# The first half of k loaded as fp32 over two other queues, with three small edits beside it: windowed attention and a gated feed-forward on one core

## The chip, the cores and the metric

The kernel runs on one core of one Trainium2 chip. The metric is the device time of one execution in microseconds (us); of several executions the median counts.

## The reference

The inputs are fp32: q, k and v of 8 batches, 8 heads, 576 positions and head size 64, and two weights.

```python
scores = q @ k.T / sqrt(64)                       # per batch and head
scores = where(|i - j| <= 32, scores, -1e9)       # a window of 32 to each side
x = (softmax(scores) @ v), heads side by side     # 4608 tokens x 512
h = x @ w_in                                      # 512 -> 2048
g = where(h >= 1, h, where(h <= -1, 0, (h + 1)**2 / 4))
out = g @ w_out                                   # 2048 -> 512
```

## The kernel before

**Two jobs in one stream.** All work is in bf16. Attention makes xT, the normalized attention output with tokens along the columns, batch by batch. The feed-forward goes over blocks of 256 tokens (18 blocks) in eight steps of 256 hidden columns. The main loop counts these steps as `a` (a = 8 x block + step): each does eight hp matmuls (L504), then ScalarE and VectorE turn hp into gT (L508 to L516). Attention pieces are hung between the steps by a table written by hand, `at(a, ...)`; each engine runs its instructions in the order in which the program gives them.

**The product with w_out** for the first two blocks is cut into sixteen pieces, `pair(x)` (L460): piece x = 0 to 3 takes block 0, output columns 0 to 255, and w_out rows 512x to 512x + 511 (row groups k = 4x to 4x + 3). The list `pairs` says behind which step a each piece goes.

**Loads.** The inputs come in by DMA. GpSimd issues nearly all of them, and these DMAs cast fp32 to bf16 on the way: `load_half` (L85), `load_v` (L106), `load_w_in` (L110), `load_w_out` (L115), `load_rows` (L92) and `load_nat` (L98). GpSimd's order is: the first half of batch 0's k, two DMAs; the small mask operation (L131); v of batch 0, four DMAs; w_in columns 0 to 511, four; the second half of q and k, four; w_in on; w_out rows k = 0 to 3; the last w_in; three mask copies (L151, L153); the rest of w_out's first 256 columns, and batch 1. [...]

**The first stretch** up to step a = 0 is a chain: load q and k, transpose them on TensorE (L187 for tiles in two parts, 18 matmuls; L189 for a cast tile, 9), copy them out of PSUM (L190, one part on ScalarE and one on VectorE), scores (L206 masks, L227 products), exponentials on ScalarE (L235), sums and products with v (L293), 1/sum by a logarithm and an exponential on ScalarE (L299, L300), the product on VectorE (L305), then hp. Idle places of TensorE are filled with dummy matmuls (L336).

Of the kernel before, what the change touches and what calls it, by code (L numbers as in the profile page):

```python
# [7 lines left out]
FP = mybir.dt.float32  # L8
# [6 lines left out]
def kernel(  # L15
# [19 lines left out]
    nc = tc.nc  # L35
    B, H, S, D = q.shape
# [40 lines left out]
    qn, kn, vn = {}, {}, {}  # L77
    HD = (slice(0, 64), slice(64, 128))

    def load_half(half, t, h, eng=None, x=None):  # L80

        src, dst, nm = ((q, qn, "qh"), (k, kn, "kh"))[t]
        if (0, half) not in dst:
            dst[0, half] = early.tile([128, 2, S], BF, name=nm, tag=nm, bufs=2) if x is None else x
        (eng or nc.gpsimd).dma_start(out=dst[0, half][:, h], in_=src[0].rearrange(  # L85
            "(h y) (l p j) d -> h l p y (j d)", h=2, l=2, p=32)[h][half])
# [29 lines left out]
                            in_=moe_w_out.rearrange("(ko ki) f -> ki ko f", ki=128)[:, k0:k1, 256 * c:256 * c + 256])  # L116

    early = ctx.enter_context(tc.tile_pool(name="early", bufs=1))
    q32 = early.tile([128, 2, S], FP, name="q32")
    for h in range(2):  # L120
        load_half(0, 0, h, (nc.sync, nc.scalar)[h], q32)
    for h in range(2):
        load_half(0, 1, h)
    A.preload_act_table_set("natural_log_exp_and_others")
    warm = const.tile([128, 512], BF, name="warm")
    V.memset(warm, 0.0)
# [15 lines left out]
    def put(todo):  # L142
        for fn, *x in todo:
            fn(*x)
# [7 lines left out]
    for m, n, x in ((mask4, 8, 128), (mask8, 4, TAIL)):  # L152
        P.tensor_copy(m.rearrange("p (n j) -> p n j", n=n),  # L153
                      band[:, :x].rearrange("p (n j) -> p n j", n=1).to_broadcast([128, n, x]))
    put([(load_w_out, 0, k, k + 4) for k in range(4, 16, 4)] + [(load_rows, 1, t) for t in range(2)])
    put([(load_v, 1, n) for n in range(4)] + [(load_w_out, 1, 8 * n, 8 * n + 8) for n in range(2)])
    put([(load_nat, 2, t) for t in range(2)] + [(load_v, 2, n) for n in range(4)])

# [3 lines left out]
    def qkT(b, t):  # L162
        if t == 0:
            return qTs[b % 3][:, PAD:]
        if b not in kT:
            kT[b] = ktp.tile([128, NY * S], BF, name="kT")
        return kT[b]

    def tpose(b, n, t, copy, ps):


        half, part = divmod(n, 2)
        j0, j1 = ((0, 5), (5, 9))[part]
        if b:
            src = qn[b] if t == 0 else kn[b]
            src = [src[:, half + 2 * h] for h in range(2)]
            dst = qkT(b, t).rearrange("d (y e p j) -> d y e p j", y=2, e=2, j=9)[:, half, :, :, j0:j1]
            like = "d j (e p) -> d e p j"
        else:
            src = (qn, kn)[t][b, half]  # L180
            src = src if src.shape[1] == 9 else [src[:, h] for h in range(2)]
            dst = qkT(b, t).rearrange("d (y l p j) -> d l y p j", l=2, p=32, j=9)[:, half, :, :, j0:j1]
            like = "d j (p y) -> d y p j"
        for j in range(j0, j1):
            if isinstance(src, list):
                for h in range(2):
                    nc.tensor.transpose(ps[HD[h], j - j0], src[h][:, D * j:D * j + D], ident)  # L187
            else:
                nc.tensor.transpose(ps[:, j - j0], src[:, j], ident)  # L189
        return lambda: copy(dst, ps[:, :j1 - j0].rearrange(like, p=64 if b else 32))  # L190
# [20 lines left out]
    def scores(b, ys, pars, cs, eng, pool=ps_s, w=128):  # L211

        if b not in pt:
            pt[b] = ptp.tile([128, 2, 2, 2, 512], BF, name="pt")
        ps = two_banks(pool)
        n = 0
        if eng is None:
            cols = (ys[1] - ys[0]) * (pars[1] - pars[0]) * (cs[1] - cs[0])
            add_mask([ps[:, h] for h in range(2)], cols, w)
        for y1 in range(*ys):  # L220
            for par in range(*pars):
                for c2 in range(*cs):
                    c = 2 * c2 + par
                    for a in range(2):
                        for h in range(2):
                            s0 = S * (y1 + 2 * a) + 64 * c
                            nc.tensor.matmul(ps[HD[a], h, w * n:w * n + w], kT[b][HD[h], s0:s0 + 64],  # L227
                                             qTs[b % 3][HD[h], PAD + s0 - 32:PAD + s0 - 32 + w],
                                             start=eng is not None, stop=True, skip_group_check=True)
                    n += 1  # L230
        p = pt[b][:, :, ys[0]:ys[1], pars[0]:pars[1], 128 * cs[0]:128 * cs[1] - 128 + w]
        m = 2 if n > cs[1] - cs[0] else 1
        p = p[:, :, ys[0] - ys[0]] if ys[1] - ys[0] == 1 else p[:, :, :, 0]
        like = "p h (y j) -> p h y j"
        A.activation(p, ps[:, :, :w * n].rearrange(like, y=m), AF.Exp, scale=D ** -0.5)  # L235
        mask(eng, p, mask4[:, :256 * n].rearrange("p (h j) -> p h j", h=2).rearrange(like, y=m))
# [81 lines left out]
    def tp1(pool):  # L318
        if pool is ps_h:
            return pool.tile([128, 8, 128], BF, name="tp", tag="hp")  # L320
        return pool.tile([128, 2, 8, 128], BF, name="tp", tag="bb")[:, 0]
# [10 lines left out]
    def keep_warm(n, pool, tag):  # L332

        z = pool.tile([128, 512], FP, name="z", tag=tag)
        for _ in range(n):
            nc.tensor.matmul(z, warm[:, :128], warm, start=True, stop=True)  # L336

    def cast(x, nm, cut):

        y = early.tile([128, 9, 2, D], BF, name=nm)  # L340
        o, i = y.rearrange("p j h d -> p h j d"), x.rearrange("p h (j d) -> p h j d", d=D)
        V.tensor_copy(o[:, :, :cut], i[:, :, :cut])
        A.copy(o[:, :, cut:], i[:, :, cut:])
        return y.rearrange("p j h d -> p j (h d)")

    with tc.tile_pool(name="ps_p", bufs=1, space=bass.MemoryType.PSUM) as ps_p:
        keep_warm(11, ps_h, "hp")

        V.memset(qkT(0, 0).rearrange("d (y s) -> d y s", y=NY)[:, :, S // 2:352], 0.0)
        for b in range(LONG):  # L350
            V.memset(qkT(b, 0).rearrange("d (y s) -> d y s", y=NY)[:, :, S - PAD:], 0.0)
        V.memset(qkT(0, 1).rearrange("d (y s) -> d y s", y=NY)[:, :, S // 2:320], 0.0)
        qn[0, 0] = cast(q32, "qb", 5)
        qq = [tpose(0, n, 0, (A.copy, V.tensor_copy)[n], tp1(ps_h)) for n in range(2)]
        for x in qq:
            x()
        kk = [tpose(0, n, 1, (A.copy, V.tensor_copy)[n], tp1((ps_n, ps_p)[n])) for n in range(2)]
        keep_warm(3, ps_h, "hp")
        for x in kk:
            x()  # L360
        scores(0, (0, 1), (0, 2), (0, 2), None)
        scores(0, (0, 2), (0, 1), (2, 3), None, ps_n, 32)
        scores(0, (1, 2), (0, 2), (0, 2), None, ps_p)
        keep_warm(4, ps_h, "hp")
        e0 = sums(0, 0, 0, TB)
        keep_warm(2, ps_h, "hp")
        e1 = sums(0, 1, 0, TB, ps_p)
        keep_warm(7, ps_h, "hp")
        e0()
        e1()  # L370
# [4 lines left out]

    NB = NT // TB
    NF = DFF // 256
    pairs = [(6, 0), (7, 1), (9, 2), (10, 3), (11, 4), (12, 5), (15, 6), (15, 8), (16, 7), (17, 9)]
    two_on_act = (1, 7, 8, 9, 10, 11, 12)
    ev = {}  # L380

# [100 lines left out]
    for a in range(NF * NB + NF):  # L482
        t, f = divmod(a, NF)
# [70 lines left out]
```

The softmax here doesn't subtract the row's maximum and nothing guards it: scores larger than these inputs give would overflow.

## Time and profile before

| | |
|---|---|
| median of 6 runs | 309.28 us (308.47 to 309.68) |
| the profiled execution | 309.21 us |
| its span, first to last instruction | 307.4 us, so 1.81 us lie around it |
| TensorE (PE) busy | 299.5 us, 97% |
| VectorE (DVE), ScalarE (ACT), GpSimd (POOL) busy | 242.1, 192.8, 77.4 us |

In timelines a row gives its start, its length, engine, line, operation, out<-in, count, and in brackets the idle time of the engine before it with what ended that. PEld are weight loads, POOL rows of DMA are issues (the transfer lands later), and DMA rates count the bytes written, so that a transfer that casts fp32 to bf16 reads twice the rate shown.

### The profile page before, as it was taken

To read this page: it belongs to the slowest core of one execution; us is meant where nothing else is said; L and a number is where in the kernel's file an instruction comes from. 1 tells how busy PE (TensorE), PEld (TensorE's weight loads), DVE (VectorE), ACT (ScalarE), POOL (GpSimd) and SP (SyncE) were. 2 spreads that over 40 slices of the span, in tenths; PEclk is the share of its full clock that TensorE was granted. 3 is DMA by queue.
4 is the path that set the end of the run, shared out by engine and by line. 5 is a ranking of instruction groups with operands and counts; after the bars stand their busy time and mean duration, and the time that the engine had idled before them with its cause. 6 is when DMAs were issued, how large, how long until landed. Compare 5 with 4: busy or idle time off the path is not lost.

```text
span 307.4 us, 8496 instructions
## 1 busy us (share of the span) xinstructions
PE 299.5 (97%) x3650; PEld 206.4 (67%) x3650; DVE 242.1 (79%) x376; ACT 192.8 (63%) x320; POOL 77.4 (25%) x92
## 2 busy tenths in 40 slices
PE   7979999999999999999999999999999999999995
PEld 3558878876666666666666666666666666666654
DVE  4278568978888888889888888889888888888760
ACT  4687886747856667566656666566676666554431
POOL 8798461018007205500460003700000000000000
PEclk9999999999999999999999999999999999999999
DMA  9999999999999997996799056990820011010111
GB/s 150 183 194 189 179 201 155 170 161 130 146 210 80 169 190 93 172 99 143 106 169 136 33 107 98 163 146 28 170 56 36 34 36 36 35 36 34 58 47 68
DMA packets 137174, 35.70 MB, mean 116 GB/s; under 512 B 122161, under 2 KB 132913, under 8 KB 137137
## 3 DMA queue, kind: packets, MB, share of 16 engines
q0 software_dynamic: 102976, 18.06, 82.6%
q1 hardware_dynamic: 34016, 16.81, 25.6%
q8 instruction: 28, 0.46, 0.6%
q10 hardware_dynamic: 144, 0.29, 0.4%
q14 instruction: 10, 0.07, 0.1%
HBM read 36.70 MB, written 9.44 MB: 150 GB/s over the span
## 4 chain that ended last, share of the span: by engine, by line
PE 90%; DMA 4%; POOL 3%; ACT 1%; issue 1%; DVE 0%; POOLq 0%; ACTq 0%
PE hp L504 39%; PE op L444 36%; PE bb L293 6%; PE op L460 4%; DMA w_in<-in_moe_w_in_dram 4%; PE bb L227 2%; PE op L433 1%; POOL vn L106 1%; POOL w_in L110 1%; PE tp L187 1%; ACT pt L235 1%; POOL kh L85 0%; DVE gT L513 0%; ACT mx L512 0%; PE bb L252 0%
## 5 line engine op out<-in xcount | busy, mean ns | idle before, releaser
L504 PE MATMUL hp<-xT,w_in 128*128 128x256 bf16 x1152 | 149.4, 273 | 2.4 <-DMA w_in<-in_moe_w_in_dram 1.1
L508 ACT ACTIVATE rr<-hp 128x512 f32<-128x512 f32 x144 | 85.7, 595 | 88.6 <-PE hp L504 88.5
L504 PEld LDWEIGHTS <-w_in 128*128 128x128 bf16 x1152 | 112.0, 98 | 41.8 <-issue 2.3
L444 PE MATMUL op<-w_out,gT 128*128 128x512 bf16 x496 | 126.9, 380 | 0.0
L515 DVE TENSOR_TENSOR mx<-hp,rr 128x512 f32<-128x512 f32 x137 | 94.5, 689 | 31.1 <-ACT rr L508 29.2
L516 DVE SCALAR_TENSOR_TENSOR gT<-rr,mx 128x512 bf16<-128x512 f32 x137 | 95.2, 695 | 4.7
L444 PEld LDWEIGHTS <-gT 128*128 128x128 bf16 x496 | 46.1, 98 | 34.8
L98 POOL DMA_DIRECT2D qn<-in_q_dram x12 | 14.6, 1223 | 111.7 <-DMA kT<-kn 107.7
L235 ACT ACTIVATE pt<-bb 128x1024 bf16<-128x1024 f32 (+1 forms) x33 | 32.7, 1002 | 4.6 <-PE bb L227 3.2
L305 DVE TENSOR_TENSOR xT<-bb,rc 128x512 bf16<-128x512 f32 (+1 forms) x32 | 21.0, 657 | 10.2 <-ACT rc L300 9.6
L106 POOL DMA_DIRECT2D vn<-in_v_dram x32 | 27.5, 893 | 4.9 <-DMA w_out<-in_moe_w_out_dram 3.7
L300 ACT ACTIVATE rc<-lr 128x512 f32<-128x512 f32 (+2 forms) x40 | 23.5, 587 | 1.3
L449 ACT COPY osb<-op 128x512 f32<-128x512 f32 x31 | 18.1, 583 | 8.7 <-PE op L444 8.3
L299 ACT ACTIVATE lr<-bb 128x512 f32<-128x512 f32 (+2 forms) x40 | 22.0, 551 | 0.4 <-PE bb L293 0.4
L201 DVE TENSOR_TENSOR pt<-pt,mask 128x1024 bf16<-128x1024 bf16 (+1 forms) x33 | 20.2, 613 | 0.5 <-ACT pt L235 0.5
L293 PE MATMUL bb<-pt,ones 64*64 64x256 bf16 (+3 forms) x352 | 19.6, 256 | 0.1
L293 PE MATMUL bb<-pt,vn 64*64 64x128 bf16 (+3 forms) x712 | 18.4, 204 | 0.2 <-DMA vn<-in_v_dram 0.2
L293 PEld LDWEIGHTS <-vn 64*64 64x64 bf16 x712 | 16.7, 107 | 0.4 <-DMA vn<-in_v_dram 0.4
L460 PE MATMUL op<-w_out,gT 128*128 128x256 bf16 x128 | 16.5, 273 | 0.0
L293 PEld LDWEIGHTS <-ones 64*64 64x64 bf16 x352 | 10.2, 105 | 8.9 <-issue 8.9
L98 POOL DMA_DIRECT2D kn<-in_k_dram x12 | 14.6, 1234 | 0.2
L460 PEld LDWEIGHTS <-gT 128*128 128x128 bf16 x128 | 12.0, 98 | 1.9
(59 smaller groups left out, 115.5 us busy)
## 6 DMA issues: line engine op xcount, KB each, us to landing
out_dram<-osb SPq DMA_DIRECT2D x35, 256.0 KB, 2.4
vn<-in_v_dram POOLq DMA_DIRECT2D x32, 144.0 KB, 10.5
qn<-in_q_dram POOLq DMA_DIRECT2D x12, 288.0 KB, 7.0
kn<-in_k_dram POOLq DMA_DIRECT2D x12, 288.0 KB, 9.4
w_in<-in_moe_w_in_dram POOLq DMA_DIRECT2D x12, 128.0 KB, 6.1
w_out<-in_moe_w_out_dram POOLq DMA_DIRECT2D x4, 256.0 KB, 7.3
w_out<-in_moe_w_out_dram POOLq DMA_DIRECT2D x2, 512.0 KB, 15.4
kh<-in_k_dram POOLq DMA_DIRECT2D x4, 144.0 KB, 5.3
```

Source lines behind the costliest of these rows:

```text
L98: nc.gpsimd.dma_start(out=x[:, :, h], in_=src[b, NY * h:NY * h + NY].rearrange("y s d -> (y s) d") .rearrange("(u p) d -> p u d", p=128))
L106: nc.gpsimd.dma_start(out=vn[b][64 * a:64 * a + 64, :, h], in_=v[b, y:y + 2].rearrange("y s d -> (y s) d") .rearrange("(c r) d -> r c d", ...
L235: A.activation(p, ps[:, :, :w * n].rearrange(like, y=m), AF.Exp, scale=D ** -0.5)
L293: nc.tensor.matmul(bb[HD[h], a, o + c0:o + c1], ones[HD[a]] if c is None else vn[b][HD[a], c, h], p(a, h), start=n == 0, stop=True, skip_g ...
L299: A.activation(lr[:, :, :D0], bb[:, :, D0:2 * D0], AF.Ln)
L300: A.activation(rc[:, :, :D0], lr[:, :, :D0], AF.Exp, scale=-1.0)
L444: nc.tensor.matmul(o, gT[tt // 2][:, j, 128 * (tt % 2):128 * (tt % 2) + 128], w_out[:, j], start=not done, stop=len(done) == 2 * NF - 1, s ...
L460: nc.tensor.matmul(o[:, tt], gT[p][:, j, 128 * tt:128 * tt + 128], w_out[:, j, 256 * half:256 * half + 256], start=not done, stop=len(done ...
L504: nc.tensor.matmul(hp[:, j], w_in[:, kk, 256 * f + 128 * j:256 * f + 128 * j + 128], xT[:, kk, r0:r0 + TB], start=n == 0, stop=n == 3)
L508: A.activation(rr, hp, AF.Relu, scale=0.5, bias=0.5)
L515: V.tensor_max(mx, hp, rr)
L516: V.scalar_tensor_tensor(g, rr, 1.0, mx, op0=ALU.min, op1=ALU.mult)
```

## The change

Four edits. The first half of batch 0's k is loaded like q's: as fp32 into k32, one DMA on SyncE's queue and one on ScalarE's, each behind q's DMA there, and a second `cast` makes the bf16 tile kb, after q's cast and before q's copies in the order of VectorE and ScalarE; its transposes are 9 instead of 18. GpSimd's two k DMAs are gone, so v's are its first. The loads of w_out rows k = 8 to 11 and 12 to 15 (columns 0 to 255) become one DMA. Piece 1 of the w_out product goes behind step a = 8 instead of a = 7.

```diff
-    q32 = early.tile([128, 2, S], FP, name="q32")
-    for h in range(2):
-        load_half(0, 0, h, (nc.sync, nc.scalar)[h], q32)
-    for h in range(2):
-        load_half(0, 1, h)
+    q32, k32 = [early.tile([128, 2, S], FP, name=nm) for nm in ("q32", "k32")]
+    for t, x in enumerate((q32, k32)):
+        for h in range(2):
+            load_half(0, t, h, (nc.sync, nc.scalar)[h], x)
...
-    put([(load_w_out, 0, k, k + 4) for k in range(4, 16, 4)] + [(load_rows, 1, t) for t in range(2)])
+    put([(load_w_out, 0, 4, 8), (load_w_out, 0, 8, 16)] + [(load_rows, 1, t) for t in range(2)])
...
         qn[0, 0] = cast(q32, "qb", 5)
+        kn[0, 0] = cast(k32, "kb", 5)
...
-    pairs = [(6, 0), (7, 1), (9, 2), (10, 3), (11, 4), (12, 5), (15, 6), (15, 8), (16, 7), (17, 9)]
+    pairs = [(6, 0), (8, 1), (9, 2), (10, 3), (11, 4), (12, 5), (15, 6), (15, 8), (16, 7), (17, 9)]
```

## The prediction

> **What bounds the kernel now.** I read the page's busy times first: PE is busy 97% of the span, so only PE's few idle places can be won. Next come PE's own waits (who, for what, us in total, times, longest):
>
> ```profile
> PE hp L504 <- DMA w_in<-in_moe_w_in_dram: 1.1, 1, 1.1
> PE hp L504 <- DVE gT L513: 1.0, 2, 0.6
> ...
> PE bb L293 <- DMA vn<-in_v_dram: 0.2, 1, 0.2
> ```
>
> Apart from the start of the dummy matmuls, the largest is one wait for w_in. The chain that ended last (start, length, what) shows where it comes from:
>
> ```profile
> 3.03 3.34 POOL vn L106 x4
> 6.37 1.77 POOL w_in L110 x3
> 8.14 6.41 DMA w_in<-in_moe_w_in_dram
> 14.55 0.28 issue
> 14.84 1.20 POOL w_in L110 x2
> 16.04 7.08 DMA w_in<-in_moe_w_in_dram
> 23.12 0.14 issue
> 23.26 1.03 PE hp L504 x8
> ```
>
> The chain runs through GpSimd's loads to step a = 4, whose w_in lands at 23.12; PE starts 0.14 later. From there to the end it is almost all PE. So the change pays if, and only if, it moves a = 4 or delays something after it. The timeline shows the part that the change rewrites:
>
> ```profile
> 5.12 0.73 DVE L342 CAST qb<-q 128x640 bf16<-128x640 f32 x1 [1.05 <-DMA q<-in_q_dram]
> ...
> 6.39 0.76 ACT L190 COPY qT<-tp 128x640 bf16<-128x640 bf16 x1 [0.67 <-PE tp L189]
> ...
> 6.51 0.91 PE L187 MATMUL tp<-ident,kh 128*64 128x128 bf16 x18
> ...
> 7.45 0.73 DVE L190 COPY kT<-tp 128x512 bf16<-128x512 bf16 x1
> ...
> 11.27 0.60 ACT L299 ACTIVATE lr<-bb 128x512 f32<-128x512 f32 x1 [0.36 <-PE bb L293]
> ...
> 23.26 0.38 PE L504 MATMUL hp<-xT,w_in 128*128 128x256 bf16 x2 [1.06 <-DMA w_in<-in_moe_w_in_dram]
> ```
>
> k is not waited for: its transposes follow q's at once. Last, busy time by window (the final two numbers are the busy share of the DMA engines and GB/s written):
>
> ```profile
> 3.00:4.00 1.00, 1.00 (x4) 0.33 (x3) 0.90 (x7) 0.00 (x0) 1.00 (x3) 1.00 0.89 286
> 6.00:9.00 3.00, 3.00 (x75) 1.98 (x78) 1.47 (x2) 1.72 (x3) 3.00 (x6) 1.00 2.93 147
> 10.00:22.00 12.00, 10.59 (x213) 7.10 (x213) 6.57 (x9) 8.93 (x16) 10.19 (x17) 1.00 1.34 196
> ```
>
> From 10 to 22 us the engines write 196 GB/s, that is read 392, without a break: w_in arrives late because the transfers ahead of it fill the engines, not because GpSimd issues late.
>
> **GpSimd's queue.** Two k issues go (1.26 us in the timeline). The mask operation needs step, set at 1.41, so v starts near 1.9 instead of 2.94: all GpSimd loads are issued some 1.05 us earlier. What it is worth at a = 4 lies between 1.05 (if issue set the pace) and 0 (if the engines do). I take 0: k's 2 x 288 KB of reads still stand ahead of v, and the rate is flat. It may even cost: k now is written as fp32: its 590 KB take 1.5 us at the 392 of the cast reads and 2.1 at the 286 GB/s of the stretch from 3 to 4 us, which holds the start of q's transfer too; so 0 to 0.6 us more, and I take **+0.1**, near the steady row. The range is -0.3 to +0.5: w_in's landings are ragged (mostly 0.6 to 0.8 us apart, but 1.85 ahead of 14.55 and 2.18 ahead of 23.12).
>
> [...]
>
> **k's own path.** q's DMAs, issued at 0.74, land at 5.02 (4.3 later) and 4.43. k's are issued behind them, near 1.4. Its 590 KB at 286 to 392 GB/s behind q's 5.02 lands at 6.5 to 7.1; if v's packets, now moving from about 4.5, take half of the engines, near 8.0. I take 6.7, since a v packet (128 bytes) is short beside one of 2304. Before, k landed at 6.68, but ready in bf16. Now VectorE goes: cast 0.73 from 6.78, then q's copy 0.73, then k's copy 0.73 with small gaps: end 9.01 instead of 8.18, **+0.83**. q's copies, ready at 6.39, wait behind the cast on both engines; that is what is queued behind the new wait. PE's 9 fewer transposes lie beside this. The exponentials then end at 11.74 instead of 10.91. L299, which started at 11.27 because v landed at 10.68, starts at 11.76: v's wait covers 0.34 of the 0.83, and a = 0 comes **+0.49** later. That then meets the 1.06 us for which PE waits at a = 4: **0** on the end. On ScalarE the cover is 0.28 idle at 24.05 and 0.98 at 28.0, enough too. Without the cover it costs 0.49; it is gone once k lands after about 7.3.
>
> **w_out in one piece.** One issue less (0.75 us) on a queue that the engines bound: 0. But rows k = 8 to 11, which piece 2 reads at 31.89, landed at 29.85; as part of the merged DMA they land with k = 12 to 15, at 31.52. With the 0.14 from landing to matmul the slack falls from 1.9 to 0.23 us. Landings scatter by several tenths: I take **+0.1**, range 0 to +0.7.
>
> **Piece 1 behind a = 8.** The same 0.87 us of PE, moved. Step a = 9 waits until 31.02 for VectorE (L513 of a = 7), which starts from a = 7's hp and does not move: the idle 0.33 stays. The slack of w_out k = 4 to 7 (landed 28.55, read at 28.78) grows by 0.87. Nothing waited there in this execution: **0**, range -0.2 to +0.1.
>
> **Sum.** 0.1 + 0 + 0.1 + 0 = +0.2 on the profiled 309.21 (span 307.4 and 1.81 around it); the median is 0.07 above it. 309.28 + 0.2 = **309.5 us**; with its terms' spread 309.0 to 309.9.
>
> **Rivals.** *k comes late (slower).* The fp32 k shares the engines evenly with v and lands at 8.0: a = 0 comes 0.49 + 1.3 = 1.8 later, the 1.06 at a = 4 covers the rest up to +0.73; with the other +0.2 this is 310.2, and 310.9 if the merged w_out is late by 0.7 as well. It decides from a landing at 7.3 on. For it: v is issued 1.05 earlier, into k's way, and v's small packets hold the engines long (busy share 2.93 at 147 GB/s). Against: packets of 2304 bytes should get most of the bytes. *Only w_out is late:* +0.7 there, 310.0. *The early queue is what counts (faster).* w_in for a = 4 lands up to 1.05 earlier; PE is ready at 22.2 + 0.49, so it gains at most 0.57 there; piece 2 then hits the merged w_out unless that moves too: -0.25 to -0.8, 308.5 to 309.0. For it: the chain does start with GpSimd issues. Against: the flat rate. *The change doesn't do what it says:* v is issued first but its packets move behind k's all the same; that is my own case.
>
> **How the numbers follow.** The measurement can tell about 0.2%, 0.62 us. My case and the small gains hold 0.42 within that; the late k 0.29 and the late w_out 0.10 make slower 0.39; faster by over 0.62 needs the early queue nearly whole: 0.19. For 8 in 10 the range reaches to the larger gain, 308.6, and the late pair, 310.9.
>
> **What would show it.** Right: k32 lands near 6.7, kT's copies end near 9.0, a = 0 starts near 15.0, w_in for a = 4 still lands at 22.9 to 23.5 and PE's wait before it shrinks from 1.06 to about 0.6; piece 2 starts with no or a short wait for w_out. Wrong: k's cast after 7.4 with no wait left at a = 4 (slower), or w_in for a = 4 before 22.6 (faster). A granted clock below 1.00, which no window shows now, would break all of it.

## The result: slower by 0.3%, and in two kinds of executions

The changed kernel took a median of 309.25 us (308.54 to 313.28, 40 runs), the kernel before 308.73 us (308.41 to 309.86, 82 runs). The ratio is 1.0032 (95% interval 1.002 to 1.0043), that is 0.99 us. It is larger than the 0.52 us between the medians because the time after has a tail: of 41 executions, the profiled one among them, 29 lie at 308.54 to 309.75 (median 309.07, granted clock 0.999 or 1.000) and 12 at 311.00 to 313.28 (mean 312.16; eleven with a mean granted clock of 0.989 to 0.995, one with 0.998). The kernel before has nothing above 309.86. I call the first kind *common* and the second *late*; in the experiments an execution counts as late above 310.5 us. The ratios leave out two late executions as disturbed, the one at 313.28 and one at 314.34 in experiment 3.

The profile after shows a late execution: 312.35 us, with a span of 310.5. Between the loads and the casts the changed kernel's lines have numbers one lower: its L188, L189, L292, L335 and L341 are L189, L190, L293, L336 and L342 of the kernel before. On its page:

```profile
span 310.5 us, 8483 instructions
...
PEclk9799999999999999999999999999999999999999
```

The row PEclk has a 7 in its second slice: TensorE's granted clock fell there, near 8 to 15 us. The chain that ended last (start, length, what) now begins with k instead of with GpSimd's loads:

```profile
1.46 7.44 DMA k<-in_k_dram
8.90 0.03 issue
...
8.99 0.50 DVE kb L341
9.50 0.05 issue
9.54 0.88 PE tp L188 x9
...
17.75 0.70 DVE xT L304
18.45 0.04 issue
18.50 1.58 PE hp L504 x13
```

k lands at 8.90, and a = 0 (the last line) starts at 18.50, where the prediction had 15.08. PE's own waits (who, for what, total, times, longest) have no w_in any more. The largest is new:

```profile
PE tp L188 <- DVE kb L341: 2.7, 1, 2.7
...
PE hp L504 <- DVE xT L304: 0.5, 1, 0.5
PE hp L504 <- DVE xT L307: 0.4, 1, 0.4
```

q's copies stand behind kb's cast on both engines: q's transposes ended at 6.81, and the copies began at 9.40 on VectorE and 9.50 on ScalarE. The busy times by window (length; busy time and instructions of PE, its weight loads, VectorE, ScalarE and GpSimd; granted clock; DMA share; GB/s) show what that wait brings with it:

```profile
6.44:9.85 3.41, 0.69 (x12) 0.51 (x11) 0.86 (x2) 0.87 (x2) 1.39 (x3) 1.00 2.89 142
9.87:13.28 3.41, 3.41 (x54) 1.76 (x55) 0.96 (x2) 1.50 (x3) 2.51 (x5) 0.50 1.47 191
13.28:20.00 6.72, 6.27 (x105) 3.69 (x97) 1.41 (x3) 4.67 (x8) 5.99 (x11) 1.00 1.29 183
```

In the 3.41 us that hold the wait, PE is busy for 0.69. In the next 3.41 us PE is busy throughout, but at a clock of 0.50. Then the clock is 1.00 again, to the end.

### The profile page after: what moved, and what is told of

The parts are those of the page before. It is cut to its first block, busy times and chain, and to the rows that moved or that the text cites. A ratio compares the mean times of both kernels' runs of the same rounds, so it can differ in the third digit from the quotient of the medians.

```text
span 310.5 us, 8483 instructions
## 1 busy us (share of the span) xinstructions
PE 301.3 (97%) x3641; PEld 207.5 (67%) x3641; DVE 241.8 (78%) x377; ACT 192.8 (62%) x321; POOL 75.5 (24%) x89
## 4 chain that ended last, share of the span: by engine, by line
PE 90%; ACT 3%; DMA 2%; DVE 2%; issue 1%; SPq 0%; ACTq 0%; DVEq 0%
PE hp L504 39%; PE op L444 35%; PE bb L292 6%; PE op L460 4%; PE bb L226 2%; DMA k<-in_k_dram 2%; PE op L433 1%; ACT pt L234 1%; PE z L335 1%; PE tp L186 1%; DVE xT L304 1%; ACT rc L299 1%; ACT lr L298 1%; PE bb L205 0%; DVE mx L515 0%
## 5 line engine op out<-in xcount | busy, mean ns | idle before, releaser
L444 PEld LDWEIGHTS <-gT 128*128 128x128 bf16 x496 | 46.1, 98 | 34.8
L292 PE MATMUL bb<-pt,ones 64*64 64x256 bf16 (+3 forms) x352 | 19.6, 255 | 0.2
L292 PE MATMUL bb<-pt,vn 64*64 64x128 bf16 (+3 forms) x712 | 18.2, 204 | 0.0
L292 PEld LDWEIGHTS <-vn 64*64 64x64 bf16 x712 | 16.7, 107 | 0.0
L292 PEld LDWEIGHTS <-ones 64*64 64x64 bf16 x352 | 10.3, 105 | 8.9 <-issue 8.9
L226 PE MATMUL bb<-qT,kT 64*64 64x128 bf16 (+1 forms) x520 | 13.5, 221 | 0.3 <-DVE kT L189 0.2
```

The lines of the kernel that those rows point to most:

```text
L292: nc.tensor.matmul(bb[HD[h], a, o + c0:o + c1], ones[HD[a]] if c is None else vn[b][HD[a], c, h], p(a, h), start=n == 0, stop=True, skip_g ...
L444: nc.tensor.matmul(o, gT[tt // 2][:, j, 128 * (tt % 2):128 * (tt % 2) + 128], w_out[:, j], start=not done, stop=len(done) == 2 * NF - 1, s ...
```

## Experiments

**1. The changed kernel again, unaltered** (no edit).

> The changed kernel once more, unaltered, to see an execution of the common kind. Of its 40 executions so far 29 took 308.5 to 309.8 us and 11 took 311.0 to 313.3; the profiled one was of the second kind (312.35). All theories: about a quarter of the executions above 310.5, the others near 309.0. A profile of the common kind should show k's last semaphore step before 7.3 us (8.90 in the late kind), the cast of k right after it, the granted clock at 1.00 or close to it, and PE waiting for w_in again at step a = 4 (23.1 to 23.4). If the common kind has PE waiting for neither k nor w_in, the extra 0.3 us over before's 308.73 must lie behind a = 4.

309.26 us, ratio 1.0026 (1.0001 to 1.0052); two of 11 executions were late: 311.5 (clock 0.994) and 313.21 (0.989). This time the profile caught a common one (309.30 us). Its timeline:

```profile
6.96 0.57 DVE L341 CAST kb<-k 128x640 bf16<-128x640 f32 x1 [1.28 <-DMA k<-in_k_dram]
...
8.31 0.72 DVE L189 COPY kT<-tp 128x512 bf16<-128x512 bf16 x1
...
15.10 1.69 PE L504 MATMUL hp<-xT,w_in 128*128 128x256 bf16 x14 [0.45 <-DVE xT L304]
...
22.64 1.05 PE L504 MATMUL hp<-xT,w_in 128*128 128x256 bf16 x8
```

So k lands at 6.94 here, kT's copy ends at 9.03, a = 0 starts at 15.10 and a = 4, the last line, at 22.64. PE waited 0.6 us for kb, and the clock stayed at 1.00. Unlike what was expected, PE doesn't wait for w_in at a = 4: it landed at 22.13.

**2. The kernel before again** (no edit), for a common execution to set beside it: the before profile shown ahead of the prediction, 309.21 us, belongs to the slower quarter of the kernel before's executions (20 of 82 lie at 309.2 or above).

> The kernel before once more, for a second profile. Of its executions about a quarter took 309.2 to 309.9 us, as the profiled one (309.21), the others 308.4 to 309.0. In one of the faster kind I expect w_in for step a = 4 to land near 22.2 us instead of 23.12 and PE to wait for it by less than 0.3 us instead of 1.06: then the cover that the prediction counted on is there in the slower executions alone.

308.74 us, close to the median of 308.73. Its timeline:

```profile
14.77 1.69 PE L504 MATMUL hp<-xT,w_in 128*128 128x256 bf16 x14 [0.43 <-DVE xT L305]
...
22.31 1.05 PE L504 MATMUL hp<-xT,w_in 128*128 128x256 bf16 x8
...
30.52 1.03 PE L504 MATMUL hp<-xT,w_in 128*128 128x256 bf16 x8 [0.62 <-DVE gT L513]
```

The second line is a = 4. It has no bracket: its w_in landed at 21.94 and PE came later, at 22.31. The wait of 1.06 us on which the prediction built goes with the slower quarter: the other profile of such an execution, 309.33 us in experiment 8, has it too (1.13 us at a = 4). Against this execution, the common one of the change is 0.33 us late at a = 0 (15.10 - 14.77) and still 0.33 us late at a = 4 (22.64 - 22.31): nothing covers it.

**3. Only the k edit**, with w_out's loads and `pairs` as before. The diff is against the kernel before.

```diff
-    q32 = early.tile([128, 2, S], FP, name="q32")
-    for h in range(2):
-        load_half(0, 0, h, (nc.sync, nc.scalar)[h], q32)
-    for h in range(2):
-        load_half(0, 1, h)
+    q32, k32 = [early.tile([128, 2, S], FP, name=nm) for nm in ("q32", "k32")]
+    for t, x in enumerate((q32, k32)):
+        for h in range(2):
+            load_half(0, t, h, (nc.sync, nc.scalar)[h], x)
...
+        kn[0, 0] = cast(k32, "kb", 5)
```

> Only the k edit: k as fp32 over two queues with its cast, v first on GpSimd; the w_out loads and piece 1 as in the kernel before. Theory 1 (the k edit makes all of the loss): as the changed kernel, a quarter of the executions above 310.5, the others near 309.0. Theory 2 (the late kind is the k edit's, but the 0.3 us of the common kind is the merged w_out's): still a quarter above 310.5, the others near 308.7, as before.

309.04 us, ratio 1.0017 (1.0002 to 1.0033), three of 12 executions above 310.5: 310.59 (clock 0.994), 310.96 (0.993) and 314.34 (0.989). The late executions are there with this edit alone. For the small loss of the common ones it says less: the other nine have a median of 308.98, and the kernel before, run beside it, 308.81. In its profiled execution (310.16 us) k landed at 7.17, PE waited 1.4 us for kb, and the clock stayed at 1.00.

**4. Only the w_out edits**, with k as before. The diff is against the kernel before.

```diff
-    put([(load_w_out, 0, k, k + 4) for k in range(4, 16, 4)] + [(load_rows, 1, t) for t in range(2)])
+    put([(load_w_out, 0, 4, 8), (load_w_out, 0, 8, 16)] + [(load_rows, 1, t) for t in range(2)])
...
-    pairs = [(6, 0), (7, 1), (9, 2), (10, 3), (11, 4), (12, 5), (15, 6), (15, 8), (16, 7), (17, 9)]
+    pairs = [(6, 0), (8, 1), (9, 2), (10, 3), (11, 4), (12, 5), (15, 6), (15, 8), (16, 7), (17, 9)]
```

> Only the w_out edits: rows k = 8 to 15 in one DMA and piece 1 behind a = 8; k over GpSimd's queue as before. Theory 1 (the k edit makes all of the loss): 308.7, as before, none above 310. Theory 2 (merged w_out late for piece 2): 309.0, with PE waiting 0.1 to 0.5 us for w_out before piece 2 near 31.9 us.

308.81 us, ratio 1.0000 (0.9992 to 1.0009), no execution above 309.5. In its timeline:

```profile
28.53 1.03 PE L504 MATMUL hp<-xT,w_in 128*128 128x256 bf16 x8 [0.16 <-DVE xT L308]
...
31.33 1.04 PE L460 MATMUL op<-w_out,gT 128*128 128x256 bf16 x8
```

The last line is piece 2. It doesn't wait: the merged w_out landed at 30.94. With piece 1 gone from behind a = 7, the next step, a = 8 (first line), comes 0.16 us before its xT; a = 9's wait for L513, 0.62 in experiment 2, is gone in exchange. So the w_out edits cost nothing that this comparison can tell (its interval ends at 0.28 us), and the loss belongs to k.

**5. v held back**: three more mask operations on GpSimd ahead of v, their output unused, so that v is issued at 3.32 instead of 1.84. This was to test whether k is late because v's packets run into it. The diff is against the changed kernel.

```diff
+    hold = early.tile([128, 257], BF, name="hold")
+    for n in range(3):
+        P.affine_select(out=hold, in_=step, compare_op=ALU.is_ge, fill=-1.0, base=-65, channel_multiplier=-1,
+                        pattern=[[1, 257]])
```

> The changed kernel with three more mask operations of 0.41 us on GpSimd ahead of v's loads (their output is not used), so that v is issued near 3.0 us as in the kernel before, not at 1.84. Theory A (v's many small packets collide with k's fp32 packets on one DMA engine): the late kind is gone or rare, k's last semaphore step falls before 7 us, no execution above 310.5, median near 308.9. Theory B (k as second DMA on its queue lands late in some executions whatever v does): a quarter still above 310.5 and PE's wait for k's cast still over 2 us in those.

309.94 us, ratio 1.0047 (1.0017 to 1.0077), and four of 8 executions late: 310.6, 311.44, 311.6 and 312.24 us. A later issue of v doesn't make k any safer. But the edit moved only the issue of v, not its transfer. v's rows (issue times, then the time from issue to landing), first of experiment 1, then of this kernel:

```profile
L106 POOL DMA_DIRECT2D vn<-in_v_dram x4: 866/881/977, 1.8 to 4.5; - x4
DMA to landing us min/median/max: 6.4/6.6/6.9
```

```profile
L106 POOL DMA_DIRECT2D vn<-in_v_dram x4: 866/881/977, 3.3 to 6.0; - x4
DMA to landing us min/median/max: 4.5/4.7/4.8
```

Issued 1.5 us later, v takes 1.9 us less to land. Its first packet moves at 5.33 us here and at 5.43 in experiment 1. So the experiment doesn't test the collision with v, which stays open.

**6. Six dummy matmuls between q's transposes and k's**, put into the changed kernel. PE then has work while it waits. Run twice.

```diff
+        z = two_banks(ps_s)
+        for _ in range(6):
+            nc.tensor.matmul(z[:, 0], warm[:, :128], warm, start=True, stop=True)
```

> The changed kernel with six more dummy matmuls (some 1.3 us at full clock) on TensorE between q's and k's transposes, so that TensorE idles less while it waits for k's cast. Theory H (the idle place before k's transposes makes the clock gate take one 3.4 us window at half clock; that is what the late executions cost): none above 310.5, every mean clock at 0.998 or more, median near 309.0. Theory L (k itself lands 2 us late in some executions, and the clock is only a consequence): still a quarter above 310, now at full clock, some 1.5 us over the others.

> e4 again (the changed kernel with six dummies), for more executions beside the changed kernel on the same chip: none below a mean clock of 0.998, a tenth to a quarter above 310 from a late k, the others near 309.1.

309.22 us, ratio 1.0015 (1.0003 to 1.0027), one of 12 executions above 310.5 (310.88, clock 0.999); the second time 309.29 us, 1.0019 (1.0 to 1.0037), and one of 12 (312.38, clock 0.995, which the expectation had excluded). That is 2 of 24, where the unaltered changed kernel has 18 of 64 (12 of 41, 2 of 11, and 4 of 12 in experiment 10; 310.28 and 310.02 us lie between the two kinds and aren't counted). Worked out at that rate, 2 or fewer of 24 would come up about 2 times in 100. The dummies are no help to k's landing where that was compared (9.84 with dummies, 9.71 without, in experiment 9). In the second kernel's profile k landed at 7.58, PE's wait was 0.5 us and the clock stayed at 1.00. Theory H was read off the late profile, where PE waits 2.7 us and 3.41 us at a clock of 0.50 follow (9.87 to 13.28); that the one brings on the other was my guess when this was run.

**7. k32 loaded by GpSimd**, as fp32 and ahead of v; cast on chip as in the change (diff against the changed kernel).

```diff
-            load_half(0, t, h, (nc.sync, nc.scalar)[h], x)
+            load_half(0, t, h, ((nc.sync, nc.scalar)[h], nc.gpsimd)[t], x)
```

> The changed kernel with k32 loaded by GpSimd, ahead of v as in the kernel before, but as fp32 and with the cast on chip: only the queue is put back. Theory L (the second DMA on each of the two queues is what comes late): none above 310.5, median near 309.0. Theory H (cast and idle TensorE suffice): a quarter still above 310.5 with a mean clock near 0.994.

309.22 us, ratio 1.0013 (1.0003 to 1.0024); none of 11 executions above 310.12, all clocks 0.998 or more. In its profile (308.85 us) k landed at 6.61; a = 0 started at 14.89 and a = 4 at 22.43, each 0.12 later than in experiment 2, and the time is 0.11 longer. The tail goes when k leaves the two queues (at a rate of 18 in 64, none of 11 would come up about 3 times in 100). A small loss stays. The cast on chip and the wait for it are the likely cause; no run separates them from the fp32 k's larger transfer on this queue.

**8. A second, unused cast of q32** in the kernel before, to price the place that a cast takes.

```diff
         qn[0, 0] = cast(q32, "qb", 5)
+        cast(q32, "db", 5)
```

> The kernel before with q's cast made twice (the second copy is not used): VectorE is held 0.73 us and ScalarE 0.62 us where the changed kernel casts k, while k comes over GpSimd in bf16 as before. If step a = 4 covered a delay of the first stretch, as the prediction had it: 308.7, no change. If the cover is missing in most executions: 309.0 to 309.3, as the common executions of the changed kernel, and the sums of batch 0 (L293) or step a = 4 come 0.3 to 0.6 us later. Theory H: some executions above 310.5 at a clock of 0.994; theory L: none.

308.73 us, ratio 0.9996 (0.9986 to 1.0007). The test missed its aim in part: its data being there already, the extra cast ran at 5.78 to 6.70, in time that was idle before, and q's copies weren't delayed. It shows that the work of a cast costs nothing there. The cost of *waiting* for k with q's copies queued behind wasn't copied by it.

**9. k late in every execution, without and with dummies.** GpSimd loads v in the order v, v, k, k, v, v, with k32 as fp32; the second kernel adds 12 dummy matmuls where experiment 6 has six. The diff, against the changed kernel, is the first's.

```diff
-    for t, x in enumerate((q32, k32)):
-        for h in range(2):
-            load_half(0, t, h, (nc.sync, nc.scalar)[h], x)
+    for h in range(2):
+        load_half(0, 0, h, (nc.sync, nc.scalar)[h], q32)
...
+        if n == 1:
+            for h in range(2):
+                load_half(0, 1, h, nc.gpsimd, k32)
```

> The kernel of e5 (k32 over GpSimd's queue, cast on chip) with k made late on purpose: GpSimd issues two of v's DMAs, then k's two, then v's other two. The engines stay busy and v's end hardly moves; k should land near 8.5 us instead of 6.6, in every execution. Theory H+L (a late k makes TensorE idle over 2 us, and that trips the clock gate): most executions at 311 to 313 with a mean clock of 0.993 to 0.995, like the late executions of the changed kernel. If a late k costs only itself: all near 310.5 to 311 at a clock of 0.999 or more.

> e8 with twelve dummy matmuls (some 2.6 us at full clock) between q's and k's transposes. Theory H+L: the clock stays at 0.999 or more, and the time shows the late k alone, 310.4 to 311.0. If the clock is not what makes the difference: as e8.

Without dummies: 313.59 us (313.35 to 314.5), ratio 1.0164 (1.0148 to 1.018), every clock 0.988 to 0.995. With them: 311.83 us (311.49 to 312.47), ratio 1.0097 (1.0082 to 1.0112), every clock 1.000. k landed at 9.71 and 9.84. PE's wait and the two windows around it, first without dummies, then with:

```profile
PE tp L190 <- DVE kb L343: 3.6, 1, 3.6
```

```profile
7.69:11.10 3.41, 0.74 (x10) 0.66 (x11) 1.16 (x3) 1.31 (x3) 2.75 (x6) 1.00 1.86 197
11.10:14.51 3.41, 3.27 (x55) 1.63 (x55) 0.70 (x1) 1.71 (x4) 2.61 (x6) 0.50 1.35 198
```

```profile
PE tp L190 <- DVE kb L343: 0.7, 1, 0.7
```

```profile
7.69:11.10 3.41, 2.73 (x19) 1.34 (x18) 1.13 (x2) 1.18 (x3) 2.76 (x6) 1.00 1.85 212
11.10:14.51 3.41, 3.25 (x89) 1.85 (x88) 0.73 (x1) 2.71 (x5) 2.67 (x6) 1.00 1.36 198
```

With PE busy for 0.74 of one window, the next runs at 0.50 and holds 55 matmuls; with 2.73 busy it runs at 1.00 and holds 89. This takes the two prices apart. The clock: 313.59 - 311.83 = 1.76 us, about half of the window of 3.41. The lateness: 311.83 - 309.22 (experiment 7) = 2.61 us for a landing 3.23 later (9.84 against 6.61); both kernels took longer than expected, with k landing over 1 us after the 8.5 aimed at. The 1.76 may be a little high for one window: the profiled execution without dummies lost one and has a mean clock of 0.994, but three of the five have 0.988 or 0.989, twice as far below 1, as if they had lost two. None of these was profiled.

**10. The changed kernel a third time**, for more executions and a second late profile.

> The changed kernel again, on the same chip as e4b: a quarter of the executions above 310.5, nearly all of these at a mean clock below 0.996; the others near 309.1.

309.12 us, ratio 1.0034 (1.0008 to 1.006), four of 12 executions late (310.73, 311.17, 311.8, 312.85). The profile shows one at 311.8 us: k's two halves landed at 8.31 and 7.92, PE waited 2.3 us for kb, and the clock was 0.50 from 9.43 to 12.85.

No kernel here beat the one before; experiments 4 and 8 equal it.

## Why the prediction was right, and where its steps were not

The forecast was 309.5 us, and 0.2 us over the median that it started from. The measured loss is larger, 0.52 us by the medians and 0.99 by the ratio, but 309.25 lies inside the range by luck, because the starting value was high: over 82 runs the kernel before has 308.73, not the 309.28 of the six runs. By the bound of 0.62 us that the prediction set for the measurement, the ratio makes the change slower, the case with a chance of 0.39, and not unchanged (0.42), its likeliest. Step by step:

- **GpSimd's queue, 0 to +0.1: right.** w_in for a = 4 landed at 21.94 in the common execution of before (experiment 2) and at 22.13 in that of the change; at 22.07 to 22.22 in experiments 4, 5 and 7. Issues 1.1 us earlier (v from 1.84 instead of 2.94) bought nothing, and the trace shows why: v's first packet moved at 5.43 in experiment 1 and at 5.47 in experiment 2. As the prediction had it, v is issued earlier but moves no earlier. Where w_in lands about 1 us later (23.20 in experiment 3's profile), the slower quarter of the kernel before has that too. The sign that the prediction set for "faster" (before 22.6) was met all the same, since the reference of 23.12 came from the slower quarter. For k's own landing the queue did matter: 6.61 over GpSimd's (experiment 7), against 6.94 over the two others in a common execution and 8.90 in a late one.
- **k's own path, in common executions: right.** Landing 6.7 forecast, 6.94 seen (v's packets moving from 5.43, not from about 4.5; in the trace before, a v packet of 128 bytes took 0.03 us at the middle value, one of q's of 2304 bytes 0.09); kT's copies end at 9.01 and 9.03; a = 0 at 15.08 and 15.10. Against the common execution of before the delay is 0.33, not 0.49, because that one starts a = 0 at 14.77 and not at 14.59.
- **"0 on the end" for that delay: this step failed.** It took the 1.06 us wait at a = 4 as cover. Experiment 2 shows that the cover is not there in an execution at the median; the 0.33 us of a = 0 arrives whole at a = 4. The prediction's own fallback, "without the cover it costs 0.49", was the right line: experiment 7, which has the cast but no tail, measures +0.4 us (0.1 to 0.7 by its interval), and the median of the 29 common executions of the change lies 0.34 us above that of before (their means are 0.22 apart). Not all of it is explained: in experiment 1's profile PE also loses some 0.6 us between a = 5 and a = 6, 0.40 of it as a wait at L292 that the profile puts down to "issue", and gets 0.29 of it back at a = 9. Experiment 3 has 0.76 us at the same instruction, experiments 2 and 7 none. No run was made on that.
- **Merged w_out +0.1 and piece 1 at 0: right, the first a little high.** Experiment 4: 1.0000 (0.9992 to 1.0009). In experiment 1 the merged load landed at 30.42 and piece 2 ran at 32.08, without a wait. The slack was not 0.23 but 0.4 to 1.7 us.
- **The rival "k comes late": right in direction, wrong in mechanism and price.** It put the landing near 8.0, and in the two late profiles k's four halves land at 7.92 to 8.90; 18 of 64 executions were late. That this share, 0.28, is near the chance of 0.29 is luck: the chance was for the kernel as a whole, not for a part of its executions. The landing at which it was to decide, 7.3, wasn't tested closely (common profiles without dummies end at 7.17). But k's landing marks don't look like an even share with v. In the late profile the half on SyncE's queue had 15 of its 16 landing marks by 6.85 and the last at 8.90; ScalarE's had 15 by 5.69 and the last at 8.41. So one mark of 16 is late in each half, and the casts wait for it (8.98 and 8.99); what stands behind that mark the trace doesn't name. In the second late profile (experiment 10) the half on SyncE's queue had 12 marks by 5.36 and the other four from 6.32 to 7.92.
- **The price of the late case was missed**, 310.2 to 310.9 against 311.0 to 313.3. The prediction's last sentence named what it left out, a granted clock below 1.00, and gave it no price. Between the common profile (experiment 1) and the late one, a = 0 moves by 18.50 - 15.10 = 3.40 us: about 2.0 is k's landing (8.90 against 6.94), and half of a 3.41 us window, 1.7, is the clock; the two together, 3.7, are near it. Two late executions, 311.00 us (clock 0.998) and 310.73 (0.999), show the lateness without a half-clock window. At the end 312.35 - 309.30 = 3.05 is left. Experiment 9 is the direct evidence that these are two costs and how large each is.

What stays open is why one or a few of k's landing marks are late on these queues in about a quarter of the executions. Loading k from GpSimd instead (experiment 7) ended it in 11 of 11 executions, so it is tied to the second DMA behind q on the SyncE and ScalarE queues, or to when that moves; what held them up isn't shown. v's packets are a rival that no run excludes: in the late profile they move from 5.47, while the last of k is under way. Against v as the start of it: one packet of k took 1.02 us from 4.83 there, and in the second late profile one took 1.67 us from 4.84 (the middle value is 0.09), both begun before v's first packet.

## What to carry to other kernels

Before calling a delay covered, see whether the covering wait is there in an execution at the median: one profile can come from the slower quarter, and its largest wait may be just what makes it slow (here 1.06 us in the execution of 309.21 us, none at that place in the one of 308.74). When a load is moved to where its landing can slip by 2 us, count what its waiter does meanwhile: here a landing 3.23 us later cost 2.61 us with 12 dummy matmuls on TensorE, and 1.76 us more, at a clock of 0.50 for 3.41 us, without them (experiment 9). When some executions of a kernel are 1% longer than the rest, look at the PEclk row of one of them before looking for a slower engine.

## What was not expected of the hardware

**The clock fell to half behind waits of 2.3 to 3.6 us.** Three profiles have PE waiting 2.3 (experiment 10), 2.7 (the late profile) and 3.6 us (experiment 9 without dummies) for kb; in each the clock is 0.50 in a following stretch of 3.41 us. Those with waits of 0.5 to 1.4 us stay at 1.00. In the late profile PE was busy for 0.69 of the 3.41 us ahead of the drop, and did nothing but transposes there:

```profile
6.18 0.63 PE L188 MATMUL tp<-ident,qb 128*128 128x128 bf16 x6
9.54 0.56 PE L188 MATMUL tp<-ident,kb 128*128 128x128 bf16 x6 [2.73 <-DVE kb L341]
```

In the other two the window ahead holds 1.13 and 0.68 us of transposes and at most 0.11 us of anything else. In experiment 3, with a wait of 1.4 us, the stretch around it (5.48 to 8.89, the first 3.41 us of its clock record) holds 0.6 us of dummy matmuls beside the transposes, and the clock stayed. These profiles differ in how long PE idles and in what it does in the rest of the stretch; no run here separates the two.

**Two DMAs were late by one of their 16 landing marks.** In the late profile each half of k had 15 of its 16 before 6.94, when the common profile has all of k; the last came at 8.41 and 8.90, up to 2 us later.
